# Attention feeding a gated FFN on one core: transposes and output products one slot later, three sets of exponentials, another order of the score tiles, an earlier load of q and k

## The chip, the cores and the metric

One Trainium2 chip, one of its cores. The metric is device time in microseconds (us) of one launch: the median of several runs. Instructions are named by engine: TensorE (PE in the profile; PEld is its weight load), VectorE (DVE), ScalarE (ACT), GpSimd (POOL), SyncE (SP, which here only issues DMAs).

## The reference

```python
def _attn_ref(q, k, v):                       # 8 x 8 heads, 576 positions, 64 wide
    scores = scale * np.matmul(q, k.transpose(0, 1, 3, 2))
    mask = block_i >= block_j                 # causal over blocks of 64
    scores = np.where(mask, scores, -1000000000.0)
    scores = scores - np.max(scores, axis=-1, keepdims=True)
    attn = np.exp(scores)
    attn = attn / (np.sum(attn, axis=-1, keepdims=True) + 1e-09)
    return np.matmul(attn, v).astype(np.float32)

def _moe_ref(x, w_a, w_b, w_out):             # x: 4608 x 512, w: 512 x 1536, 1536 x 512
    a = x @ w_a
    b = x @ w_b
    return (a * b @ w_out).astype(np.float32)
```

The attention's output, heads side by side, is x. The weights of the FFN come as 64-bit floats, and the kernel converts them to pairs of a high and a low 32-bit part; most matrix products are made of three products of such parts.

## The kernel before

The kernel has two stages. The first is the **attention loop**, a loop over *slots* s, one for each of the 64 heads and LAG = 2 more. In it the attention is the main thread, and a first pass of the FFN (features 0 to 3 of 12, `first_pass`) is strewn between its steps as *filler*: single matmuls of 288 columns (line 217). The second stage, behind the loop, does the other features (`pair_unit`, `pair_out`, lines 708 and 754), while VectorE converts their weights. The change touches nothing in the second stage.

Three generators make a head i:

- `softmax(i)`: a side block (line 412, 128 x 128) and four tiles of scores (line 392: `last`, of 512 columns, and t = 0, 1, 2 of 192, 320 and 448); VectorE masks them (lines 413, 414, 430) and takes the maxima (398, 420, 421); ScalarE makes the exponentials (line 401: `e`, and `e_s` of the side block) with their sums. The side block lies in the same PSUM tile as score tile 1 (`p1`), of which the pool `ps_sc` has three. A last step sums and inverts (lines 435 to 442, `rc`) and has GpSimd normalise the exponentials in place (line 445). The exponentials lie in NE = 2 sets of buffers, used in turn (`i % NE`).
- `turn(i)`: the transposes of the exponentials on TensorE in four steps, t = 3, 2, 1, 0 (line 468, `tp`), ScalarE's copy of each (line 470, `ah`) and VectorE's remainder (line 472, `al`).
- `values(i)`: the output products with v in two steps (lines 517 to 523, `av`), their sums (lines 527 to 532), and for every odd head the split of x into high and low parts (`xh`, `xl`).

The first 8 heads (NATIVE) use plain fp32 matmuls without the split into parts. A slot runs through a table of steps: which generator, for which head relative to s, and how many thirty-sixths of a slot's filler follow it. `now` is the slot number with that fraction. `want(now)` says how many filler matmuls are to be issued by then: it begins at MOE_FROM = 10.2 and reaches 36 a slot from slot 18 on. The conversion of the first pass's 12 weight parts (`convert_w`, lines 139 to 149 on VectorE, with ScalarE and GpSimd) is paced by `n_conv`: one part a slot, five steps each. `KEEP` adds idle matmuls in slots 0 and 1.

q and k of a pair of heads come by `load_pair` (lines 321 and 322, one buffer each behind the first four pairs), are scaled and split by `split_q` and `split_k`, and are spread to both halves of the partitions by four DMAs a head in `spread` (lines 358 and 359). All these are issued by SP in one queue, together with the loads of v (line 330), of weights (line 124), and the partial outputs (line 555).

The order in which an engine gets its instructions is not exactly that of the program: a scheduler takes, of those that it holds to be ready, the one that was written first. `behind_of` pins an instruction behind another in its queue, without a wait.

Of the kernel before, what the change touches and what calls it, by code (L numbers as in the profile page):

```python
# [23 lines left out]
CONV_PER_SLOT = 1.0  # L24
CONV0 = 1
HL_DVE = False
MOE_FROM = 10.2
# [6 lines left out]
NATIVE = 8  # L34
SPARE = 8
# [17 lines left out]
def attention_then_bilinear_ffn(  # L53
# [10 lines left out]
    nc = tc.nc  # L64
    B, H, D, S = kT.shape
# [217 lines left out]
    NE = 2  # L283
# [90 lines left out]
    def softmax(i):  # L374
# [51 lines left out]
        for t in range(LAST):  # L426
            ps = p1 if t == 1 else ps_sc.tile([P, 512], F32, tag="sc", name=f"s{t}{n}")
            mark = scores(t, ps)

            nc.vector.memset(ps[:BLK, nk[t] - BLK:nk[t]], NEG)  # L430
            top(t, ps[:, :nk[t]])
            exps(t, es[t][:, :nk[t]], ps[:, :nk[t]], nm[:, t:t + 1])
            if t < LAST - 1 or not native:
                yield mark
# [15 lines left out]
    def turn(i):  # L450
# [8 lines left out]
        for t in range(LAST, -1, -1):  # L459
# [14 lines left out]
            if t == SIDE_T and not native:  # L474
                yield mark
                behind_of(lower(), "rc")
                continue
            if not native:
                ins = lower()
                if t == 0:  # L480
                    behind_of(ins, "rc")
# [101 lines left out]
    def want(now):  # L583

        n = (now - H - LAG) * per_slot - behind
        if now < 2 * H + LAG:
            n = (H * per_slot - behind) * (now - MOE_FROM) / (2 * H + LAG - MOE_FROM)
        return int(n)
# [6 lines left out]
    SLOT = [(S_, 0, 3), (S_, -1, 0), (T_, -2, 4), (S_, 0, 4), (V_, -2, 3), (S_, 0, 3),  # L595
            (T_, -1, 4), (V_, -2, 3), (S_, 0, 3), (T_, -1, 5), (T_, -1, 4)]
    fill = sum(m for _, _, m in SLOT)
    gens = {}
    for s in range(NH + LAG):
        p, odd = divmod(s + 4, 2)  # L600
        if p < NH // 2 and not odd:
            load_pair(p)
# [3 lines left out]
        for what, i, m in SLOT:  # L606
            i += s
            if 0 <= i < NH:
                steps.append((gens.get((what, i)) or gens.setdefault((what, i), what(i)), m))
        due = k = 0  # L610
        for g, m in steps:
            mark = next(g)
# [5 lines left out]
            marks.append(mark)  # L618
            if k == 1 and 0 < s <= NH:
                split_v(s - 1)  # L620
# [4 lines left out]
            if k == (3 if odd else 6) and s + 2 < NH:  # L625
                spread(s + 2)
            k += 1
            due += m
            now = s + due / fill
            while n_conv < 5 * int(now * CONV_PER_SLOT + CONV0):  # L630
                next(conv, None)
                n_conv += 1
# [261 lines left out]
```

## Time and profile before

| | |
|---|---|
| median of 3 runs | 1279.61 us (1277.71 to 1281.69) |
| the profiled execution | 1281.83 us, its span 1279.8 us |
| TensorE matmul busy | 1239.3 us, 97% |
| TensorE weight load busy | 1173.2 us, 92% |
| VectorE busy | 999.2 us, 78% |
| ScalarE busy | 683.6 us, 53% |
| GpSimd busy | 554.9 us, 43% |
| granted TensorE clock, mean | 0.988 |

The attention loop ends about 640 us into the span. Busy times are shares of the whole; the two stages have different limits, so a stage has to be read by itself. Ends of matmuls are modelled, so that a TensorE that shows no idle time may still issue more slowly than it could; the length of a slot, from one head's side block to the next, is the safer measure. "A <- B: x, n, m" in the waits says that A stood idle for x us in all, n times, at most m, until B was done.

### The profile page before, as it was taken

The page shows a single profiled execution, that of the slowest core. Times are in us where ns is not written, and L with a number is a line of the kernel's source. Part 1 is how long each engine was busy: PE and PEld are TensorE (multiplying, and loading weights), DVE is VectorE, ACT ScalarE, POOL GpSimd, SP SyncE. Part 2 cuts the span into 40 slices and gives each one's busy share as a digit, 9 for nine tenths or more (in the row PEclk, how much of TensorE's full clock was granted, in tenths as well). Part 3 has the DMA queues.
Part 4 walks back from the last instruction along what each step waited for, and adds up shares of the span by engine and source line. Part 5 has one row for each costly group of instructions (what it writes and reads, how often), then busy time and mean ns, then how long its engine had stood idle before and what let it go on. Part 6 is the DMA issues. An engine that isn't in the chain of part 4 may idle for free.

```text
span 1279.8 us, 23524 instructions
## 1 busy us (share of the span) xinstructions
PE 1239.3 (97%) x7849; PEld 1173.2 (92%) x7849; DVE 999.2 (78%) x2389; ACT 683.6 (53%) x1722; POOL 554.9 (43%) x679
## 2 busy tenths in 40 slices
PE   9988999999999999999988998999999999999998
PEld 5668998999999999999988998999999999999998
DVE  6878887777887877877699999899967577577553
ACT  5788787788787788888745423233222222122210
POOL 4567565566665565665422322223223123123231
PEclk8999999999999999999998999999999999999999
DMA  5467766777767767676225355364466442243131
GB/s 195 132 167 201 187 174 175 178 171 181 170 167 179 179 171 176 167 178 155 87 94 171 100 180 194 139 206 164 141 220 244 145 149 79 70 149 98 52 99 62
DMA packets 93496, 196.58 MB, mean 154 GB/s; under 512 B 11968, under 2 KB 52928, under 8 KB 93376
## 3 DMA queue, kind: packets, MB, share of 16 engines
q1 hardware_dynamic: 88768, 185.64, 51.4%
q10 hardware_dynamic: 4608, 9.44, 2.0%
q8 instruction: 63, 1.03, 0.3%
q14 instruction: 57, 0.47, 0.1%
HBM read 96.47 MB, written 47.19 MB: 112 GB/s over the span
## 4 chain that ended last, share of the span: by engine, by line
PE 71%; DVE 15%; DMA 4%; issue 4%; ACT 3%; POOL 2%; SPq 1%; ACTq 0%; DVEq 0%; POOLq 0%
PE pso_z L754 13%; PE ps L217 12%; PE tp L468 7%; PE psx_z L708 6%; PE psw_z L708 6%; PE psv_z L708 6%; PE pso L217 4%; PE s L392 4%; PE psy_z L708 3%; PE av L517 3%; PE av L523 3%; PE sl L392 2%; DMA kp<-kT 2%; PE av L507 2%; DVE sw L147 1%
## 5 line engine op out<-in xcount | busy, mean ns | idle before, releaser
L113 POOL TENSOR_TENSOR h_z<-u_z,h_z 128x384 fp32r<-128x384 f32 x96 | 112.8, 1175 | 391.4 <-ACT h_z L110 379.8
L217 PE MATMUL ps<-xh,wab 128*128 128x288 f32 x1024 | 241.8, 304 | 1.2 <-ACT a L241 1.2
L754 PE MATMUL pso_z<-h_z,wo 128*128 128x384 f32 x1152 | 204.0, 335 | 4.5 <-POOL h_z L113 4.5
L445 POOL TENSOR_SCALAR e<-e,rc 128x512 f32<-128x512 f32 (+3 forms) x256 | 151.6, 604 | 127.9 <-DVE rc L442 118.1
L754 PEld LDWEIGHTS pso_z<-h_z,wo 128*128 128x128 f32 x1152 | 199.6, 188 | 7.0 <-POOL h_z L113 7.0
L217 PEld LDWEIGHTS ps<-xh,wab 128*128 128x128 f32 x1024 | 172.3, 189 | 4.7 <-ACT a L241 1.4
L472 DVE TENSOR_TENSOR al<-tp,ah 128x512 fp32r<-128x512 f32 x224 | 131.6, 608 | 31.5 <-ACT ah L470 31.0
L217 PE MATMUL ps<-xl,wab 128*128 128x288 f32 x512 | 154.1, 301 | 0.0
L468 PE MATMUL tp<-ident,e 128*128 128x128 f32 x832 | 136.1, 278 | 10.4 <-POOL e L445 4.0
L470 ACT CAST ah<-tp 128x512 fp32r<-128x512 f32 x224 | 116.4, 531 | 50.3 <-PE tp L468 47.5
L110 ACT CAST h_z<-u_z 128x384 fp32r<-128x384 f32 x96 | 49.3, 514 | 167.7 <-DVE u_z L733 160.2
L217 PE MATMUL pso<-hh,wo 128*128 128x288 f32 x512 | 128.1, 311 | 4.3 <-ACT hh L110 4.3
L708 PE MATMUL psx_z<-xh,wab 128*128 128x384 f32 x384 | 118.5, 344 | 7.2 <-DVE u_z L726 6.7
L468 PEld LDWEIGHTS tp<-ident,e 128*128 128x128 f32 x832 | 100.8, 142 | 25.7 <-POOL e L445 9.5
L401 ACT ACTIVATE e<-s,nm 128x192 f32<-128x192 f32 (+2 forms) x192 | 101.5, 529 | 32.4 <-DVE nm L398 23.2
L708 PE MATMUL psw_z<-xh,wab 128*128 128x384 f32 x384 | 117.0, 340 | 0.8 <-DVE u_z L728 0.8
L708 PE MATMUL psv_z<-xh,wab 128*128 128x384 f32 x384 | 116.7, 339 | 0.5 <-DVE u_z L730 0.4
L398 DVE TENSOR_REDUCE nm<-s 128x1 f32<-128x192 f32 (+3 forms) x256 | 109.9, 431 | 2.4
L217 PEld LDWEIGHTS ps<-xl,wab 128*128 128x128 f32 x512 | 96.5, 188 | 3.4
L217 PEld LDWEIGHTS pso<-hh,wo 128*128 128x128 f32 x512 | 88.3, 192 | 6.6 <-ACT hh L110 5.3
L113 POOL TENSOR_TENSOR v<-vr,v 128x320 fp32r<-128x320 f32 x56 | 50.2, 897 | 89.3 <-ACT v L110 67.9
L392 PE MATMUL s<-k,q 128*128 128x256 f32 x336 | 81.2, 322 | 2.2 <-ACT e_s L401 1.9
(142 smaller groups left out, 2919.5 us busy)
## 6 DMA issues: line engine op xcount, KB each, us to landing
k<-kp SPq DMA_DIRECT2D x112, 288.0 KB, 3.8
xr<-xd SPq DMA_DIRECT2D x48, 384.0 KB, 3.5
pt<-part SPq DMA_DIRECT2D x96, 192.0 KB, 3.5
q<-qp SPq DMA_DIRECT2D x112, 160.0 KB, 2.6
raww<-wab SPq DMA_DIRECT2D x24, 512.0 KB, 3.8
qp<-qT SPq DMA_DIRECT2D x32, 320.0 KB, 3.2
vr<-vm SPq DMA_DIRECT2D x64, 160.0 KB, 3.1
kp<-kT SPq DMA_DIRECT2D x32, 288.0 KB, 3.5
```

What stands on the lines that cost most here:

```text
L110: nc.scalar.copy(hi, src)
L113: return lo_eng.tensor_tensor(lo, src, f32(hi), op=ALU.subtract)
L217: mm = nc.tensor.matmul(ps, w_, d_, start=(i == 0), stop=(i == n - 1))
L392: mark = nc.tensor.matmul(ps[:, :w], qm[:, q0[t]:q0[t] + P], kk[:, :w], start=(i == 0), stop=(i == len(ks) - 1))
L398: nc.vector.tensor_reduce(nm[:, t:t + 1], view, axis=AX.X, op=ALU.max, negate=True)
L401: nc.scalar.activation(out, view, AF.Exp, bias=bias, accum_out=sm[:, t, :1])
L445: nc.gpsimd.tensor_scalar(ev, ev, rc[:, t:t + 1], 1.0, op0=ALU.mult, op1=ALU.mult)
L468: mark = nc.tensor.transpose(tp[:, c], src, ident)
L470: nc.scalar.copy(ah[:, :m, cols], tp[:, :m])
L472: return nc.vector.tensor_tensor(al[:, :m, cols], tp[:, :m], f32(ah[:, :m, cols]), op=ALU.subtract)
L708: nc.tensor.matmul(ps, wt[:, i, iw], j[:, ix], start=start and kp == 0 and i == 0 and j is xh, stop=kp == KP - 1 and i == 1, skip_group_ch ...
L754: nc.tensor.matmul(ps, wt[:, a, osl], b, start=i == 0, stop=i == 3 * len(fs) - 1)
```

## The change

- From slot SW = 10 on another table of steps holds: all four transposes of head s − 2, and the output products of head s − 3. Before, three of the four transposes were those of head s − 1, and the products those of head s − 2. The loop has one slot more. Slots 0 to 9 keep the old table, with the first transpose and the second step of the output products exchanged.
- Three sets of exponentials instead of two.
- The score tiles come in the order last, 1, 0, 2 (before: last, 0, 1, 2), and from slot 10 on the steps of `softmax` stand 10, 7, 10 and 9 thirty-sixths apart (before 7, 7, 10 and 12).
- VectorE's remainders of the transposes are no longer pinned behind the sums (`rc`).
- The filler's pace is shifted by FFLAG = 3 slots in place of LAG = 2.
- The weight conversion goes at 0.7 parts a slot in the first 8 slots and 0.9 behind (before 1).
- `load_pair` is called in the middle of the odd slot before, instead of at the start of the even one; `split_v` a slot later.
- The scratch that GpSimd's DMAs would use is smaller.

```diff
-CONV_PER_SLOT = 1.0
+SW = 10
+FFLAG = 3.0
...
-    NE = 2
+    NE = 3
...
-        for t in range(LAST):
+        for t in (1, 0, 2):
             ps = p1 if t == 1 else ps_sc.tile([P, 512], F32, tag="sc", name=f"s{t}{n}")
...
-            if t == SIDE_T and not native:
-                yield mark
-                behind_of(lower(), "rc")
-                continue
             if not native:
-                ins = lower()
-                if t == 0:
-                    behind_of(ins, "rc")
+                lower()
             yield mark
...
-        n = (now - H - LAG) * per_slot - behind
-        if now < 2 * H + LAG:
-            n = (H * per_slot - behind) * (now - MOE_FROM) / (2 * H + LAG - MOE_FROM)
+        n = (now - H - FFLAG) * per_slot - behind
+        if now < 2 * H + FFLAG:
+            n = (H * per_slot - behind) * (now - MOE_FROM) / (2 * H + FFLAG - MOE_FROM)
...
-    SLOT = [(S_, 0, 3), (S_, -1, 0), (T_, -2, 4), (S_, 0, 4), (V_, -2, 3), (S_, 0, 3),
-            (T_, -1, 4), (V_, -2, 3), (S_, 0, 3), (T_, -1, 5), (T_, -1, 4)]
+    SLOT1 = [(S_, 0, 3), (S_, -1, 0), (T_, -2, 4), (S_, 0, 4), (V_, -2, 3), (S_, 0, 3),
+             (V_, -2, 3), (T_, -1, 4), (S_, 0, 3), (T_, -1, 5), (T_, -1, 4)]
+    SLOT = [(S_, 0, 3), (S_, -1, 0), (T_, -2, 4), (V_, -3, 3), (S_, 0, 3), (T_, -2, 4), (S_, 0, 3),
+            (V_, -3, 3), (T_, -2, 4), (S_, 0, 4), (T_, -2, 5)]
...
-    for s in range(NH + LAG):
-        p, odd = divmod(s + 4, 2)
-        if p < NH // 2 and not odd:
-            load_pair(p)
+    for s in range(NH + LAG + 1):
+        odd = s % 2
+        if s == 0:
+            load_pair(2)
...
-        for what, i, m in SLOT:
+        for what, i, m in SLOT if s >= SW else SLOT1:
...
-            if k == 1 and 0 < s <= NH:
-                split_v(s - 1)
+            if k == 1 and 0 < s - (s >= SW) <= NH:
+                split_v(s - 1 - (s >= SW))
...
+            if odd and k == 5 and s + 5 < NH:
+                load_pair((s + 5) // 2)
...
-            while n_conv < 5 * int(now * CONV_PER_SLOT + CONV0):
+            while n_conv < 5 * int(CONV0 + 0.7 * min(now, H) + 0.9 * max(now - H, 0)):
...
-    nc = bacc.Bacc("TRN2", target_bir_lowering=False, num_devices=1)
+    nc = bacc.Bacc("TRN2", target_bir_lowering=False, num_devices=1, dynamic_dma_scratch_size=1024)
```

`split_v` is called for the head one further back from slot 10 on. In slots where a generator has nothing left to do (at the change-over), its step issues nothing.

More of the change, by code (lines that the diff above doesn't have):

```diff
@@ L611, in attention_then_bilinear_ffn @@
         for g, m in steps:
-            mark = next(g)
+            mark = next(g, None)
             if not m:
@@ L617, in attention_then_bilinear_ffn @@
                 nc.tensor.matmul(keep, z[:, :P], z, start=True, stop=True)
-            marks.append(mark)
-            if k == 1 and 0 < s <= NH:
-                split_v(s - 1)
+            if mark:
+                marks.append(mark)
+            if k == 1 and 0 < s - (s >= SW) <= NH:
+                split_v(s - 1 - (s >= SW))
             if k == (3 if odd else 4) and s + 2 < NH:
```

## The prediction

> **What bounds the kernel now.** I read the page's first two parts, then the busy time of each engine slot by slot (a slot is one turn of the attention loop), then the waits, then the order of time inside two slots.
>
> ```profile
> span 1279.8 us, 23524 instructions
> PE 1239.3 (97%) x7849; PEld 1173.2 (92%) x7849; DVE 999.2 (78%) x2389; ACT 683.6 (53%) x1722; POOL 554.9 (43%) x679
> PE   9988999999999999999988998999999999999998
> DVE  6878887777887877877699999899967577577553
> PEclk8999999999999999999998999999999999999999
> ```
>
> TensorE is the bound nearly everywhere; only holes in its work can be won. The attention loop takes the first 20 of the 40 slices, and the change touches nothing behind it. So the question is how large the holes in the loop are. The slot starts (first side matmul, line 412) cut the steady part into even and odd slots of equal TensorE work. The next two rows are sums over 20 even slots (217.85 to 598.98) and the 20 odd ones between and behind them:
>
> ```profile
> sum 199.90, PE 198.10 PEld 186.66 DVE 173.34 ACT 163.82 POOL 156.53; mean PE 9.90 PEld 9.33 DVE 8.67 ACT 8.19 POOL 7.83
> ...
> sum 190.77, PE 190.77 PEld 186.22 DVE 136.02 ACT 149.23 POOL 82.50; mean PE 9.54 PEld 9.31 DVE 6.80 ACT 7.46 POOL 4.13
> ```
>
> The same matmuls take 10.00 us in an even slot and 9.54 in an odd one. I take 9.54 as TensorE's floor, since there it is never idle. The early slots, one row each, and rows that cover several, the last of them behind the loop:
>
> ```profile
> 19.72:34.81 15.09, 15.09 (x62) 9.93 (x61) 9.70 (x26) 9.08 (x26) 9.68 (x10) 0.55 0.34 108
> 42.75:54.40 11.65, 10.38 (x59) 6.80 (x58) 10.86 (x29) 8.41 (x24) 8.58 (x11) 0.85 0.57 159
> 70.82:78.60 7.78, 7.78 (x55) 5.58 (x55) 6.26 (x20) 6.86 (x20) 4.49 (x6) 1.00 0.56 191
> ...
> 106.45:119.03 12.58, 9.98 (x68) 8.64 (x67) 11.47 (x32) 8.84 (x25) 7.63 (x10) 1.00 0.73 176
> ...
> 194.78:208.29 13.51, 11.63 (x72) 10.75 (x71) 8.63 (x26) 9.09 (x26) 7.12 (x10) 0.87 0.65 172
> ...
> 6.01:97.00 90.99, 84.12 (x493) 57.01 (x492) 73.82 (x206) 66.13 (x181) 54.38 (x65) 0.91 0.55 162
> 97.00:146.77 49.77, 46.46 (x324) 42.55 (x323) 44.13 (x130) 40.94 (x112) 35.50 (x47) 1.00 0.70 191
> 97.00:175.71 78.71, 74.18 (x520) 68.47 (x518) 68.40 (x204) 63.63 (x177) 51.81 (x71) 1.00 0.71 189
> ...
> 700.00:900.00 200.00, 190.93 (x1065) 183.91 (x1065) 188.35 (x328) 70.06 (x120) 54.24 (x41) 1.00 0.51 169
> ```
>
> Columns: stretch and length, then busy time of TensorE, its weight loads, VectorE, ScalarE, GpSimd, granted clock, DMA share, GB/s. The reader is to see VectorE nearly as busy as the slot is long in 42.75 and 106.45, and the halved clock in 19.72.
>
> **The change, part by part.**
>
> *Transposes and output a slot later, three sets of exponentials (from slot 10).* In even slots TensorE waits for normalised exponentials and for the copied transposes. From the waits between 150 and 600 us:
>
> ```profile
> PE tp L468 <- POOL e L445: 1.4, 1, 1.4
> PEld av L517 <- ACT ah L470: 3.3, 20, 0.2
> ```
>
> Behind the change head i's transposes are issued in slot i+2 and its output products in slot i+3, so both inputs are about 0.6 to 0.9 slots (6 to 8 us) older when they are asked for. Both waits then have no place, and nor has the long one in slot 20. The 20 even slots give 199.90 − 190.77 = 9.1 us; slot 20 gives 13.51 − 9.54 = 4.0 us, its halved clock included. Together −13.1. What is late next is the score tile below. The third set costs three small GpSimd memsets at the start, under the first wait for q; the matmuls are the same.
>
> *Score tiles in the order last, 1, 0, 2.* Tile 1 shares its PSUM tile with the side block and waits until the side block's exponential (e_s) is done. It comes second now instead of third. An even slot and an odd slot, from the order of time:
>
> ```profile
> 413.65 0.34 PE L412 MATMUL s<-k,q 128*128 128x128 f32 x2
> 414.34 0.29 PE L217 MATMUL ps<-xh,wab 128*128 128x288 f32 x1
> 414.47 0.30 PE L217 MATMUL ps<-xl,wab 128*128 128x288 f32 x1
> 417.64 0.45 PE L392 MATMUL s<-k,q 128*128 128x320 f32 x2
> 416.69 0.37 ACT L401 ACTIVATE e_s<-s,nb 128x128 f32<-128x128 f32 x1
> ...
> 423.47 0.33 PE L412 MATMUL s<-k,q 128*128 128x128 f32 x2
> 427.15 0.45 PE L392 MATMUL s<-k,q 128*128 128x320 f32 x2
> 425.69 0.37 ACT L401 ACTIVATE e_s<-s,nb 128x128 f32<-128x128 f32 x1 [0.34 <-DVE nb L421]
> ```
>
> The slots begin with the side block at line 412. A filler matmul takes 0.13 us (414.34 to 414.47). In the odd slot e_s is done 2.59 us into the slot and tile 1 starts at 3.68; in the even one 3.41 and 3.99. Ahead of tile 1 there stand now 14 fillers, two transposes, a score tile and four output products. After the change there stand 10 fillers, four transposes and the same four products; two transposes more and a score tile less about cancel, so it is due 4 × 0.13 us sooner, at 3.1 to 3.2 us. With e_s at 2.59 nothing waits; at 3.41 TensorE would wait 0.3 to 0.4. Which of them holds is not in the trace: the even slots are late because the x split of an odd head and two late remainders of transposes run at their start, and with output a slot later that split falls at the start of odd slots, and the last transpose's remainder there is a small one. Ends: 0, and 0.4 in each of some 45 slots, 18 us. I take 2 us, near the odd row, because what made the even row late is partly gone.
>
> *Weight conversion slower in the first eight slots (0.7 parts a slot instead of 1), 0.9 behind.* By the pacing formula the 12 parts are now due at slots 0 to 11, and then at 0, 1.4, 2.9, 4.3, 5.7, 7.1, 8.4, 9.6, 10.7, 11.8, 12.9, 14.0. VectorE's five steps of the 11 parts before 97 us:
>
> ```profile
> L145 DVE SCALAR_TENSOR_TENSOR mw<-raww,mw 128x512 f32<-128x512 uint16 x11 | 9.6, 868 | 0.2
> L149 DVE TENSOR_TENSOR xw<-mw,sw 128x512 f32<-128x512 f32 x11 | 9.2, 841 | 0.5
> L147 DVE SCALAR_TENSOR_TENSOR sw<-raww,sw 128x512 int32<-128x512 int32 x11 | 8.6, 782 | 0.7 <-ACT sw L140 0.6
> L143 DVE TENSOR_SCALAR mw<-raww 128x512 int32<-128x512 int32 x11 | 8.5, 776 | 0.0
> L139 DVE TENSOR_SCALAR sw<-raww 128x512 int32<-128x512 int32 x11 | 5.6, 513 | 0.1
> ```
>
> A part costs 868 + 841 + 782 + 776 + 513 ns = 3.8 us. Slots 0 to 9 have 8 parts instead of 11, VectorE 11 us less there. TensorE lacks work for 90.99 − 84.12 = 6.9 us in that stretch and runs some 14 us at half clock (15.09 us at 0.55), which is 7 us more. Ends: −10, if the early waits that ruin the clock go, and +2, if the new order adds a wait. The first part and the first head's normalisation, which stand in front of the first hole, are unmoved, and slot 7 (70.82) is TensorE's own already. I take −3.
>
> *The change-over at slot 10.* Slots 10 to 14 get the three parts back, 11.3 us by those durations, and lose one head's transposes and outputs to later slots. VectorE's rows of these, 97 to 147 us:
>
> ```profile
> L472 DVE TENSOR_TENSOR al<-tp,ah 128x512 fp32r<-128x512 f32 x16 | 10.7, 673 | 1.1 <-ACT ah L470 1.0
> L532 DVE TENSOR_TENSOR xf<-av,avlo 64x512 f32<-64x512 f32 x5 | 3.4, 677 | 0.1
> L531 DVE TENSOR_TENSOR avlo<-avlo 64x64 f32<-64x64 f32 x5 | 3.2, 630 | 1.3 <-ACT avlo L530 1.2
> L472 DVE TENSOR_TENSOR al<-tp,ah 128x256 fp32r<-128x256 f32 x5 | 2.1, 415 | 0.0
> ```
>
> A head has 3 × 673 + 415 + 677 + 630 ns = 3.7 us of them. So VectorE has 44.1 + 11.3 − 3.7 = 51.7 us in slots 10 to 14. TensorE has less than before: the filler starts at 10.2 with 240 matmuls over 8.8 slots (27.3 a slot) instead of 7.8 (30.8). Its floor: a steady slot is 9.54, of which 36 × 0.131 = 4.7 is filler, leaving 4.8 for attention; five slots with 131 fillers make 5 × 4.8 + 131 × 0.131 = 41.2, less some 3.4 for the head that moved (24 of a slot's 34 attention matmuls), 37.8 us. VectorE becomes the bound of these slots and leaves TensorE 13.9 us without work; the buffers let it work ahead a little, and I take 13 up to slot 18. Before, the eight slots 10 to 17 (24 + 7 × 31 fillers by the old pace) had a floor of 70.2 us and took 78.71, holes of 8.5. The difference is +4.5. Ends: −2, if the extra slot of slack lets TensorE run ahead, and +10, if the clock falls as well.
>
> It can fall. The stretches around the wait in slot 20:
>
> ```profile
> 198.00:201.40 3.40, 1.75 (x11) 1.28 (x9) 2.67 (x8) 2.39 (x8) 2.48 (x2) 1.00 0.30 101
> 201.40:204.80 3.40, 3.17 (x13) 3.13 (x14) 1.05 (x4) 1.47 (x4) 2.04 (x5) 0.50 0.95 196
> ```
>
> TensorE was busy 1.75 of 3.40 us, and the next 3.40 us ran at 0.50: half idle was enough, and it cost 1.7 us. [...] The trace shows the fall after a half idle window, so I keep +10.
>
> *q and k loaded half a slot sooner.* The load is issued by SP, and SP holds it until the single buffer is free, that is, until the spreading DMAs of the pair before have landed (SP's own waits, 150 to 620 us):
>
> ```profile
> SPq L322 <- DMA q<-qp: 33.5, 25, 3.3
> SPq L321 <- DMA k<-kp: 10.5, 11, 1.9
> ```
>
> Asking sooner doesn't free the buffer, so 0. If the load's place in SP's queue shifts, a v load or a partial output behind it moves by at most the 3.3 us above, which the added slot covers.
>
> *One more slot, and the rest.* The filler's pace is shifted by the same slot (FFLAG), so the same 1968 filler matmuls are issued at the end of the loop, and the weights of the second stage find their memory free at the same point of TensorE's work: 0, with ±1.5 for a stage that VectorE's 188.35 of 200 us show to be close (row from 700 to 900). No DMA is issued by GpSimd, so its smaller scratch costs nothing.
>
> **Sum.** −13.1 + 2 + 4.5 − 3 + 0 = −9.6 us. The profiled execution took 1281.83 us (2.0 outside the span), so 1272.2 on its scale; the median of the runs is 2.2 below it, 1279.61, so **1270 us** on the median's.
>
> **The rivals.**
>
> *Tile 1 waits in every slot (slower).* The four-tile transpose now early in each slot puts a copy on ScalarE and a subtraction on VectorE ahead of e_s. If e_s is ready 0.4 to 0.5 us too late in all 45 slots, the 2 us become some 20: 1270 − 2 + 20 = 1288. It decides for slower from a mean wait of about 0.35 us. For it: the even slots' 3.41 against 3.1. Against it: e_s's chain is emitted ahead of the transpose, and odd slots have 0.5 us to spare. Chance 0.12.
>
> *The change-over eats the gain (no change, or little).* VectorE's 51.7 us plus two or three half-clock windows makes +12 instead of +4.5: 1277.5. For it: slot 11 with one part took 12.58 us at 11.47 of VectorE. Against it: the transposes behind it have a slot of slack. Chance 0.15.
>
> *The early clock holds (much faster).* With VectorE free of 11 us the holes that halve the clock in 20 to 34 us go: −11 instead of −3, 1262. Against it: the first hole's cause is unmoved. Chance 0.12.
>
> *The change does nothing in the steady slots:* the scheduler that orders each queue packs the later work just as tightly, and another wait of half a microsecond takes the place: 1279.6. Chance 0.05.
>
> **How the numbers follow.** My forecast has 0.56, with 1264 to 1276 as its own range (−13.1 to −7 steady, −2 to +10 at the change-over, −6 to +1 early, not all at one end). The range 1261 to 1282 takes in the second to fourth rival and leaves out the first. About 0.3% (3.8 us) is what a measurement of this kernel can tell from no change. Faster: 0.51 of the forecast, 0.12, and 0.05 of the change-over's, 0.68. Same: 0.05 + 0.08 + 0.05 = 0.18. Slower: 0.12 and 0.02 of the change-over's, 0.14.
>
> **What would show it.** Even and odd slots both at 9.5 to 9.6 us from slot 20 on; no wait of transposes for GpSimd's e or of output products for ScalarE's ah there; tile 1 starting near 3.1 us with e_s done before it. Slots 10 to 14 with VectorE over 90% busy, four weight parts and TensorE idle for 10 us or more. A shorter stretch before slot 10 with fewer weight steps. The stage behind the loop as long as before. The prediction is wrong if tile 1's start is pinned to the end of e_s in most slots, if the slots 10 to 14 hold no hole, or if the half-clock stretch at 20 us is gone.

## Result and the profile after

The changed kernel takes 1288.25 us in the median (1286.6 to 1293.92), the kernel before 1279.57 (1276.81 to 1281.69) beside it: a ratio of 1.0081 (95% interval 1.0062 to 1.01). It is slower by 8.7 us; 1270 was forecast, in a range of 1261 to 1282. The profiled execution took 1288.09 us. Two of the ten executions of E2 below took 2383 and 3046 us, and the only trace of E2 is of the second, so E2 has a time (the median of all ten) and no slots. The page of the changed kernel:

```profile
span 1285.9 us, 23499 instructions
PE 1231.5 (96%) x7849; PEld 1170.3 (91%) x7849; DVE 1006.2 (78%) x2389; ACT 690.8 (54%) x1723; POOL 555.7 (43%) x684
...
PE   8989899999999999999998998999999999999998
...
PEclk9999999999999999999998999999999999999999
```

The matmuls are the same 7849, TensorE is busy 8 us less (less time at half clock: the granted clock is 0.995 in the mean instead of 0.988) and the span is 6.1 us longer: more holes. Four stretches of the span add up to it. Of the kernel before (the first two of its stretches, 90.99 and 78.71 us, stand in the prediction) from slot 18 to the last output product, and from there to the end; and of the changed kernel from slot 0, 10, 19 and the last output product on:

```profile
175.71:639.38 463.67, 459.64 (x3303) 440.80 (x3302) 361.31 (x1144) 366.53 (x1026) 277.10 (x398) 1.00 0.67 167
639.38:1279.80 640.42, 616.77 (x3534) 603.80 (x3532) 494.69 (x836) 185.85 (x337) 170.22 (x132) 0.99 0.42 138
```

```profile
6.01:85.88 79.87, 74.37 (x492) 52.35 (x492) 70.47 (x199) 63.93 (x179) 51.50 (x63) 1.00 0.61 180
85.88:173.53 87.65, 77.68 (x531) 72.05 (x530) 75.25 (x227) 69.63 (x194) 56.57 (x79) 0.98 0.71 191
173.53:645.26 471.73, 457.61 (x3286) 437.82 (x3285) 364.74 (x1128) 369.90 (x1015) 275.34 (x393) 1.00 0.62 162
645.26:1285.90 640.64, 617.31 (x3538) 604.92 (x3537) 494.81 (x836) 185.84 (x337) 170.66 (x132) 0.99 0.42 138
```

Slots 0 to 9: −11.1 us. The change-over (eight slots before, nine now, with the same filler): +8.9. The rest of the loop: +8.1. The second stage: +0.2. What the early slots win is nearly given back by slot 19; the loss is made in the steady slots, where 11 us were to be won. Of the change-over, slots 10 to 14, which were to hold the most of VectorE's work:

```profile
85.88:134.86 48.98, 42.76 (x286) 38.93 (x284) 42.43 (x129) 38.35 (x105) 33.28 (x45) 0.97 0.69 194
```

The sums over the even slots 20 to 58 and the odd ones 21 to 59:

```profile
sum 207.73, PE 196.61 PEld 186.73 DVE 166.29 ACT 176.40 POOL 135.96; mean PE 9.83 PEld 9.34 DVE 8.31 ACT 8.82 POOL 6.80
```

```profile
sum 197.05, PE 194.38 PEld 186.80 DVE 150.44 ACT 144.26 POOL 104.30; mean PE 9.72 PEld 9.34 DVE 7.52 ACT 7.21 POOL 5.22
```

An even slot takes 10.39 us instead of 10.00, an odd one 9.85 instead of 9.54: now the odd slots lose too. The waits between 180 and 610 us name two things, tile 1 (line 393) behind e_s, and ScalarE behind q's load:

```profile
PE s L393 <- ACT e_s L402: 12.1, 29, 1.0
PEld s L393 <- ACT e_s L402: 20.6, 33, 1.3
ACT qp L338 <- DMA qp<-qT: 12.7, 12, 1.9
```

The last was 0.3 us in two times before. How the two hang together shows in the order of time around the start of slot 52, at 505.83 us, the longest of the steady slots (11.37 us); first ScalarE, then VectorE, then TensorE:

```profile
505.71 0.74 ACT L338 ACTIVATE qp<-qp 128x640 fp32r<-128x640 f32 x1 [1.86 <-DMA qp<-qT]
506.48 0.59 ACT L472 CAST ah<-tp 128x512 fp32r<-128x512 f32 x1
506.96 0.67 ACT L345 CAST kp<-kp 128x576 fp32r<-128x576 f32 x1
...
510.18 0.37 ACT L402 ACTIVATE e_s<-s,nb 128x128 f32<-128x128 f32 x1 [0.54 <-DVE nb L422]
```

```profile
507.10 0.69 DVE L474 TENSOR_TENSOR al<-tp,ah 128x512 fp32r<-128x512 f32 x1 [2.08 <-ACT ah L472]
507.70 0.61 DVE L399 TENSOR_REDUCE nm<-s 128x1 f32<-128x448 f32 x1
508.27 0.42 DVE L474 TENSOR_TENSOR al<-tp,ah 128x256 fp32r<-128x256 f32 x1
508.70 0.11 DVE L414 MEMSET s<- 64x64 f32 x1
...
508.92 0.62 DVE L399 TENSOR_REDUCE nm<-sl 128x1 f32<-128x512 f32 x1
509.47 0.27 DVE L399 TENSOR_REDUCE nm<-s 128x1 f32<-128x128 f32 x1
509.77 0.15 DVE L421 TENSOR_REDUCE nb<-nm 64x2 f32<-64x2 f32 x1
509.93 0.15 DVE L422 TENSOR_REDUCE nb<-nm 64x2 f32<-64x4 f32 x1
```

```profile
505.83 0.33 PE L413 MATMUL s<-k,q 128*128 128x128 f32 x2
...
507.93 0.63 PE L470 MATMUL tp<-ident,e 128*128 128x128 f32 x4 [0.86 <-DVE al L474]
...
510.69 0.56 PE L393 MATMUL s<-k,q 128*128 128x320 f32 x2 [0.52 <-ACT e_s L402]
```

ScalarE stands 1.86 us for q's load in front of the split of q; behind it waits the copy `ah` of tile 1's transpose; VectorE stands 2.08 us for that copy, because the remainder `al` of tile 1 is next in its queue, and then runs the remainder of tile 0 as well, all ahead of the maximum over the new head's `sl` (3.09 us into the slot; 0.88 in slot 47 of E11 below, where neither remainder is in front of it). So `nb`, e_s and tile 1 are late; tile 1 starts at 510.69, 0.14 us after e_s. TensorE stands twice in this slot: 0.86 us ahead of a transpose, until a remainder has freed the PSUM tile `tp`, and 0.52 us for e_s. In most of the other slots only the wait for e_s is there. In the kernel before both remainders were pinned behind `rc`, which comes after `nb`.

### The profile page after: what moved, and what is told of

Same layout as the page of the kernel before. It is cut to its first block, busy times and chain, and to the rows that moved or that the text cites. A ratio compares the mean times of both kernels' runs of the same rounds, so it can differ in the third digit from the quotient of the medians.

```text
span 1285.9 us, 23499 instructions
## 1 busy us (share of the span) xinstructions
PE 1231.5 (96%) x7849; PEld 1170.3 (91%) x7849; DVE 1006.2 (78%) x2389; ACT 690.8 (54%) x1723; POOL 555.7 (43%) x684
## 4 chain that ended last, share of the span: by engine, by line
PE 50%; DVE 19%; DMA 15%; ACT 7%; issue 5%; SPq 3%; POOL 1%; ACTq 0%; DVEq 0%; POOLq 0%
PE pso_z L756 14%; PE psx_z L710 6%; PE psw_z L710 6%; DMA k<-kp 6%; PE psv_z L710 6%; DMA kp<-kT 5%; PE ps L218 5%; PE psy_z L710 3%; PE tp L470 3%; DVE nm L399 3%; PE s L393 3%; PE pso L218 2%; DVE al L474 2%; DVE sw L148 2%; SPq L359 2%
## 5 line engine op out<-in xcount | busy, mean ns | idle before, releaser
L218 PE MATMUL ps<-xh,wab 128*128 128x288 f32 x1024 | 237.5, 301 | 0.0
L447 POOL TENSOR_SCALAR e<-e,rc 128x512 f32<-128x512 f32 (+3 forms) x256 | 162.9, 649 | 109.4 <-DVE rc L444 89.2
L474 DVE TENSOR_TENSOR al<-tp,ah 128x512 fp32r<-128x512 f32 x224 | 138.5, 619 | 29.5 <-ACT ah L472 27.5
L218 PE MATMUL ps<-xl,wab 128*128 128x288 f32 x512 | 156.9, 306 | 0.3 <-POOL xl L114 0.3
L470 PE MATMUL tp<-ident,e 128*128 128x128 f32 x832 | 133.5, 275 | 7.1 <-POOL e L447 2.5
L472 ACT CAST ah<-tp 128x512 fp32r<-128x512 f32 x224 | 119.3, 533 | 23.2 <-PE tp L470 20.2
L218 PE MATMUL pso<-hh,wo 128*128 128x288 f32 x512 | 120.3, 303 | 3.9 <-ACT hh L111 3.9
L393 PE MATMUL s<-k,q 128*128 128x320 f32 (+1 forms) x336 | 86.0, 337 | 19.1 <-ACT e_s L402 18.1
L114 POOL TENSOR_TENSOR hl<-hf,hh 128x288 fp32r<-128x288 f32 x64 | 54.5, 851 | 81.5 <-ACT hh L111 81.4
```

Of the source, the lines that this page charges most:

```text
L114: return lo_eng.tensor_tensor(lo, src, f32(hi), op=ALU.subtract)
L218: mm = nc.tensor.matmul(ps, w_, d_, start=(i == 0), stop=(i == n - 1))
L393: mark = nc.tensor.matmul(ps[:, :w], qm[:, q0[t]:q0[t] + P], kk[:, :w], start=(i == 0), stop=(i == len(ks) - 1))
L447: nc.gpsimd.tensor_scalar(ev, ev, rc[:, t:t + 1], 1.0, op0=ALU.mult, op1=ALU.mult)
L470: mark = nc.tensor.transpose(tp[:, c], src, ident)
L472: nc.scalar.copy(ah[:, :m, cols], tp[:, :m])
```

## Experiments

Times are medians; each ratio is to the kernel before, measured beside it on the same chip. "Mean" is the mean length of slots 19 to 62 in the profiled execution, and "nb" the median over these slots of the time from the slot's start to the end of `nb`; both are of one execution. Two versions that were not measured side by side are best compared by the ratio and the mean: the difference of their medians is good to a few microseconds only (the kernel before came to 1278.3 to 1280.5 us beside them).

| kernel | time, us | ratio (95%) | mean, us | nb, us |
|---|---|---|---|---|
| before | 1279.6 | 1 | 9.84 | 2.13 |
| after | 1288.3 | 1.0081 (1.0062 to 1.01) | 10.09 | 2.91 |
| E1 after, tiles last, 0, 1, 2 | 1293.3 | 1.0103 (1.0062 to 1.0143) | 10.08 | 3.53 |
| E2 before, tiles last, 1, 0, 2 | 1280.5 | 1.0001 (0.9976 to 1.0026) | – | – |
| E3 after, conversion at 1 part | 1301.5 | 1.017 (1.0125 to 1.0216) | 10.01 | 2.90 |
| E4 before, conversion at 0.7 and 0.9 | 1279.9 | 1.0 (0.9981 to 1.0019) | 9.86 | 2.13 |
| E5 after, load at the old place | 1290.7 | 1.0078 (1.0056 to 1.01) | 10.07 | 2.90 |
| E6 after, side block with tile 0 | 1290.4 | 1.0079 (1.0051 to 1.0106) | 10.08 | 3.33 |
| E7 after, old order and spacing | 1287.0 | 1.0052 (1.0037 to 1.0068) | 9.84 | 2.99 |
| E8 after, x split a step later | 1289.1 | 1.0075 (1.0053 to 1.0097) | 10.05 | 2.91 |
| E9 after, tile 0's remainder put off | 1295.3 | 1.0125 (1.0103 to 1.0147) | 10.41 | 2.45 |
| E10 old table a slot later, pins | 1288.8 | 1.0102 (1.0045 to 1.016) | 9.95 | 2.60 |
| E11 E10 and splits pinned | 1274.9 | 0.9933 (0.9902 to 0.9965) | 9.64 | 2.13 |
| E12 new spacing, pins | 1302.6 | 1.0195 (1.0146 to 1.0245) | 10.36 | 2.12 |
| E13 after, splits pinned | 1284.8 | 1.0041 (1.0019 to 1.0062) | 10.00 | 2.63 |
| E14 before, splits pinned | 1277.6 | 0.9978 (0.9965 to 0.9991) | 9.65 | 2.12 |
| E15 E1 and splits pinned | 1290.2 | 1.0073 (1.0049 to 1.0097) | 10.00 | 3.01 |
| E16 E7 and splits pinned | 1279.3 | 0.9986 (0.9965 to 1.0007) | 9.87 | 2.72 |
| E17 E11 without the pins of the remainders | 1289.0 | 1.009 (1.0056 to 1.0125) | 10.03 | 2.98 |
| E18 before without these pins | 1323.3 | 1.0339 (1.0308 to 1.0369) | 10.60 | 3.27 |

**E1, E2: the order of the tiles.**

```diff
-        for t in (1, 0, 2):
+        for t in range(LAST):
```

> The changed kernel with the old order of the score tiles (last, 0, 1, 2). Theory A (tile 1, now second, waits for the side block's exponential e_s because both lie in one PSUM tile): tile 1 is due near 5 us of a slot instead of 3.1, e_s is long done; slots 19 to 62 go from 10.09 us to 9.6, and the time from 1288 to about 1267. Theory B (the steps of older heads crowd VectorE and ScalarE, whatever the tile order): the slots stay near 10.1 and the time near 1288. Theory C (late loads of q and k hold ScalarE): only part comes back, every fourth slot stays above 10.3, about 1278.

> The kernel before with only the score tiles' order changed to last, 1, 0, 2. Theory A: tile 1 is due near 1.8 to 2.3 us of a slot and e_s is done at 2.6 (odd slots) and 3.4 (even slots), so TensorE waits some 0.7 to 1.4 us in each of 55 slots; less the old holes, 1305 to 1330. Theory B or C: within 3 us of 1279.6.

 (the same line the other way round, in the kernel before)

The order was not the cause. In E1 TensorE's matmuls wait for e_s no more, and the mean is the same 10.08: the holes stand in front of the output products and the next score tiles instead. In the kernel before, the new order does not change the time.

```profile
PE av L513 <- ACT ah L472: 6.5, 20, 0.5
PE s L393 <- ACT e L402: 2.5, 3, 1.7
```

**E6: the side block in tile 0's PSUM tile**, so that tile 1 owes e_s nothing.

```diff
-        side = p1[:, nk[1]:nk[1] + P]
+        side = p1[:, 256:256 + P]
...
-            ps = p1 if t == 1 else ...
+            ps = p1 if t == 0 else ...
```

> The changed kernel in the new order (last, 1, 0, 2), but the side block lies in tile 0's PSUM tile instead of tile 1's; nothing else moves. Theory A: tile 1 has no one to wait for, tile 0 comes third, near 5 us, behind e_s; about 1267, as in the run with the old order. Theory B: near 1288, since the order and the work are the same.

Mean 10.08, waits of transposes in place of tile 1's. With E1: take tile 1's wait away, and the next thing that TensorE asks for waits.

**E3, E4: the pace of the conversion**, in the changed kernel and in the kernel before.

```diff
-            while n_conv < 5 * int(CONV0 + 0.7 * min(now, H) + 0.9 * max(now - H, 0)):
+            while n_conv < 5 * int(now + CONV0):
```

> The changed kernel with the weights converted at the old pace, 1 part a slot. If the slower pace is what brings slot 10 from 97.0 to 85.9 us: slot 10 back near 94 to 97 us, slot 19 later than 173.5 by less than that, since the conversion is over sooner, and the time 1286 to 1292 us (0 to 3 of it kept). Rival 'the early gain is that of the third set of exponentials and of the loads': slot 10 stays at 86 to 89 us. In both the steady slots stay at 10.05 to 10.1 us, since no part of the conversion runs there.

> The kernel before with one part of the change alone: the weights converted at 0.7 part a slot in the first eight slots and 0.9 after, instead of 1. Theory 'the slower conversion is worth the whole early gain': slot 10 starts near 86 instead of 97.0 us, no half-clock stretch is left before 60 us, and the time is 1279.6 - 11 = about 1269 us (ratio 0.991). Rival 'the early gain came from the new order of loads and the extra set of exponentials': slot 10 stays near 97 us and the time within 0.3% of before. Second rival, 'the conversion comes back later': slots 10 to 25 hold more conversion and give back 4 or more of the 11 us, 1273 to 1276 us.

E3 (slot 0 to 10, slot 10 to 19), then E4 (slot 0 to 10, slot 10 to 18):

```profile
5.60:96.63 91.03, 81.52 (x492) 56.06 (x492) 74.33 (x212) 67.53 (x185) 57.37 (x65) 0.93 0.58 170
96.63:185.07 88.44, 77.90 (x531) 72.11 (x530) 70.31 (x215) 67.16 (x186) 53.17 (x77) 0.98 0.69 177
```

```profile
6.01:93.36 87.35, 84.09 (x492) 55.96 (x492) 68.10 (x200) 63.72 (x178) 46.28 (x61) 0.98 0.55 162
93.36:174.35 80.99, 74.26 (x519) 68.65 (x518) 71.12 (x210) 65.96 (x182) 56.37 (x75) 1.00 0.70 188
```

In the changed kernel the slower pace is worth 13 us by the medians and 11 by the ratios: with the old one slot 10 starts at 96.6 us again, and the change-over is no shorter. In the kernel before it wins only 3.6 us by slot 10, 1.4 of them are left at slot 18, and the time is the same: its theory fell. The other early 7 us come from the rest of the change or from the clock, which fell early in some executions and not in others: E15 and E16 have the slower pace too and differ from each other only from slot 10 on; up to there E15 ran at a clock of 0.90 and E16 at 0.98, and they began slot 10 at 92.52 and 87.74 us. Which part of the rest was not tried.

**E5, E8: the load and the x split.** E5 calls `load_pair` at the start of the even slot again. E8 puts a `yield` ahead of the split of an odd head's x and a step `(V_, -4, 0)` at the head of the table.

> The changed kernel with q and k loaded at the old place (start of the even slot). Theory C: ScalarE's waits for q's DMA (12.7 us in 180 to 610 us of the changed kernel) shrink to about 1, the slots with the longest holes (every fourth) lose some 0.6 us each, about 1281. Theory A: the load is gated by its single buffer, not by its place, so the time stays within 3 us of 1288.

> The changed kernel with the split of a pair's x (two copies of ScalarE, two subtractions of GpSimd and the store's issue on ScalarE) moved from the end of the output's second step to the start of the next slot, ahead of the side matmul. Theory 'x split': ScalarE's copies of x and the issue behind them delay e_s and the copies ah in each odd slot; moved away, odd slots lose 0.2 to 0.4 us, and the time comes to 1277 to 1283 us. Rival (pins, or the load that ScalarE waits for): odd slots stay within 0.1 us of 10.0 and the time at 1285 to 1292 us.

Neither changes anything: the load as the prediction had it (ScalarE's wait for q is 12.7 us, as after), and the theory of the x split falls.

**E7: the old order and spacing**, transposes and output still a slot later.

```diff
-        for t in (1, 0, 2):
+        for t in range(LAST):
...
+    SLOT = [(S_, 0, 3), (S_, -1, 0), (T_, -2, 4), (S_, 0, 4), (V_, -3, 3), (S_, 0, 3),
+            (T_, -2, 4), (V_, -3, 3), (S_, 0, 3), (T_, -2, 5), (T_, -2, 4)]
```

> The changed kernel with the old table of the slot and the old order of the tiles, only with every transpose at head s-2 and every output step at head s-3. Theory 'spacing': what makes the steady slots 10.1 us is that the last score tile, two transposes and the output's second step now stand close together at the slot's end; with the old spacing and the later heads the steady slots come to 9.6 to 9.85 us and the time to 1266 to 1277 us. Rival 'crowded queues whatever the spacing' (the remainder of the transposes of tile 1 and tile 0, no longer pinned behind the reciprocals, stands ahead of the maximum over the last score tile on VectorE, and ScalarE stops in its order at q's load): slots of 10.0 to 10.2 us and 1284 to 1295 us, whatever the table.

The mean is that of the kernel before, 9.84, so 0.25 us a slot belong to order and spacing together. It is not what the later transposes were to bring, `nb` is as late as in the changed kernel, and the time hardly moves: slot 19 begins 5.5 us later than in the changed kernel (179.02 against 173.53 us).

**E9, E12: the pins with the new spacing.** E9 puts off tile 0's remainder alone (a step `(T_, -3, 0)` behind `rc`). E12 has the `turn` of the kernel before, with its two pins, and the changed table with `(T_, -3, 4)` as its first transpose, so that tile 0's transpose falls at the start of the next slot.

> The changed kernel with the remainder of tile 0's transpose (VectorE, 128x256) put off to the next slot and pinned behind the reciprocals again, as in the kernel before; the remainder of tile 1 stays where the change put it. Theory 'pins': this remainder no longer stands ahead of the maximum over the last score tile; e_s's end comes 0.3 to 0.4 us sooner in a slot, tile 1's wait goes, and the time falls by 8 to 16 us to 1272 to 1280 us. Rival (the delay comes from ScalarE's queue, or from the spacing): the wait moves to another releaser and the time stays at 1284 to 1292 us.

> The changed kernel with its own order of tiles and its own spacing, but the transposes one step further on, so that tile 0's falls at the start of the next slot, and the remainders of tile 1 and tile 0 pinned behind the reciprocals as in the kernel before. Theory 'pins': the reduction over the two maxima ends at 2.1 us of a slot again instead of 2.8, e_s at 2.6 instead of 3.4, tile 1 (due at 3.15) waits in no slot, steady slots of 9.6 to 9.7 us, time 1268 to 1274 us. Rival 'spacing' (the last score tile a twelfth of a slot later, two transposes close behind it): slots stay at 10.0 or above and the time at 1284 to 1292 us.

E12 is half right: `nb` ends at 2.12 us again and tile 1 waits no more. But in the new spacing the first output step stands directly behind tile 0's transpose, and TensorE's only wait is this one:

```profile
PE av L519 <- ACT ah L472: 22.8, 39, 1.9
```

So with this table the pins cost more than they win. The splits of q and k (below) are not pinned in E12, whose slots of number 2 modulo 4 take 11.29 us and the others 9.97 to 10.09; new spacing, pins and pinned splits together were not run. E9 came out above both of its ranges: `nb` ends at 2.45 us, but the waits for e_s stay (13.4 us in 14 times). That the remainder, put off, also holds its transpose's PSUM tile longer may be why; it is not shown.

**E10, E11, E13, E14: the splits of q and k.** E10 is the changed kernel with order, spacing, pins and place of tile 0's transpose of the kernel before, all a slot later (`T_` at −3 and −2, `V_` at −3). In E11, E13 and E14 the two ScalarE copies are pinned behind e_s of the even slot:

```diff
-        exps(NT, e_s, side, nb[:, 1:])
+        last["es"] = exps(NT, e_s, side, nb[:, 1:])
...
-        nc.scalar.mul(qp[:, 1].bitcast(F32R), qp[:, 0], SCALE)
+        behind_of(nc.scalar.mul(qp[:, 1].bitcast(F32R), qp[:, 0], SCALE), "es")
...
-            nc.scalar.copy(kp[:, 0].bitcast(F32R), kp[:, 1])
+            behind_of(nc.scalar.copy(kp[:, 0].bitcast(F32R), kp[:, 1]), "es")
```

> The changed kernel with the slot of the kernel before in all but the one thing: order of tiles last, 0, 1, 2, the old spacing, tile 0's transpose at the start of the next slot, and the remainders of tile 1 and tile 0 pinned behind the reciprocals; transposes and output stay one slot later, with three sets of exponentials. Theory 'the slot later is right, what was moved along with it costs': the slots whose number is a multiple of 4 fall from 10.4 to 9.7 us, the others stay at 9.55 and 9.85, the mean comes to about 9.65, and the time to 1279.6 - 8 = 1272 us (1268 to 1276). Rival 'one slot later is itself the cost' (GpSimd's normalisation and the transposes of an older head meet the new head's work): slots of 10.0 us and more, 1284 us or above. Third, the output's later start is paid back in the change-over: 1277 to 1283 us with a steady mean under 9.75.

> The changed kernel with one order added on ScalarE: its two copies that split a pair's q and k (0.74 and 0.67 us, in the changed kernel at 9 us of an odd slot to 1 us of the next, where ScalarE stops for q's load for 1 us at a time) come behind e_s of the even slot. Theory 'splits at the boundary': these copies and the wait in front of them are what makes e_s end at 3.4 us in the slots that follow them; the wait of ScalarE for q's load goes from 12.7 us in all to under 2, slots of number 0 and 2 modulo 4 fall from 10.47 and 10.19 to about 9.9, the odd ones stay at 10.05 and 9.65, mean 9.85 to 9.95, and the time falls by 6 to 10 us to 1278 to 1282 us. Rival 'the queues are full whichever work stands there': the wait moves, slots stay at 10.05 or above, 1285 us or more.

> The kernel of 'table of before, one slot later' (1288.8 us), with the same order added: the copies that split q and k on ScalarE behind e_s of the even slot. In that kernel nearly all that TensorE loses in steady slots stands before the first transposes of every second or fourth slot, behind ScalarE's wait for q's and k's loads. Theory 'splits at the boundary': these holes go, slots of number 2 modulo 4 fall from 10.63 to 9.7, the mean from 9.95 to 9.65 or less, and the time to 1272 to 1278 us, which would be less than the kernel before. Rival 'full queues': mean above 9.85 and 1284 us or more.

> The kernel before with the same order added: here the two copies stand at 6.4 and 8.6 us of an odd slot, and go to some 3 us of the next. If the later place is free in itself: 1277 to 1281 us. If loads and spreads then come too late for the next pair, or e_s's neighbours on ScalarE are delayed: 1283 us or more, and then the place behind e_s costs in the other two kernels too.

E10 fell: a slot later, with the changed kernel's earlier load, slower conversion and third set, brought nothing. The split of q began 6.4 us after the start of an odd slot before (median), and 9.1 in the changed kernel, close to the next slot's start; pinned, it begins 3.2 to 3.3 us into the even slot. The spacing moved it, and not the load: E1 and E7 differ in the spacing alone and have it at 10.1 and 7.2 us, and E5, with the load at the old place, at 9.2. E13 won 3.4 us, less than expected. E11 won 13.9 us over E10 by the medians (1.7% by the ratios, 14.0 us in the 44 steady slots), as expected, and is the fastest version of all (its trace is of an execution of 1281.07 us, with slot 10 at 94.9 us). E14 came out a little faster than the kernel before too. Slots 19 to 62 in the kernel before, E14 and E11, one row of each:

```profile
185.25:618.10 432.85, 429.17 (x3083) 411.61 (x3082) 339.42 (x1078) 344.48 (x969) 260.52 (x374) 1.00 0.68 170
```

```profile
187.80:612.33 424.53, 423.73 (x3083) 409.39 (x3081) 349.23 (x1078) 345.66 (x969) 262.79 (x374) 1.00 0.68 174
```

```profile
180.92:604.85 423.93, 422.09 (x3083) 409.59 (x3082) 347.16 (x1079) 346.64 (x969) 261.94 (x375) 1.00 0.68 175
```

E14's transposes are as early as ever, and its steady slots are as short as E11's.

**E15, E16, E17, E18: what is left, and the pins alone.** E15 and E16 are E1 and E7 with the splits pinned. E17 is E11, and E18 the kernel before, without the pins of the remainders:

```diff
-            if t == SIDE_T and not native:
-                yield mark
-                behind_of(lower(), "rc")
-                continue
...
-                ins = lower()
-                if t == 0:
-                    behind_of(ins, "rc")
+                lower()
```

> The changed kernel with two things undone together: the order of tiles (last, 0, 1, 2, so that tile 1 comes in the middle of the slot) and the place of the splits of q and k (pinned behind e_s of the even slot). Each alone left the steady slots at 10.08 and 10.00 us. Theory 'two waits behind one another, each hidden by the other': with both gone the mean comes to 9.65 to 9.75 and the time to 1268 to 1276 us. Rival 'the new spacing and the remainders that are no longer pinned': the mean stays at 9.85 to 10.0, 1280 to 1287 us, with e_s's wait replaced by waits of transposes or of the output.

> The changed kernel with the old order of tiles, the old spacing (transposes and output a slot later, tile 0's transpose still at the slot's end) and the splits of q and k pinned behind e_s; the remainders of tile 1 and tile 0 on VectorE stay free, as the change left them. Against the kernel of 1274.9 us (slots of 9.64) it differs in these remainders and in tile 0's place alone. Theory 'the splits alone were left': mean 9.6 to 9.7, 1271 to 1278 us. Rival 'the free remainders cost': the reduction nb ends at 2.6 us or later in most slots, mean 9.75 to 9.9, 1279 to 1286 us.

> The kernel of 1274.9 us (table of before one slot later, splits of q and k behind e_s; slots of 9.64) with one thing taken out: VectorE's remainders of tile 1 and tile 0 are no longer pinned behind the reciprocals but issued at once, as in the changed kernel. Tile 0's transpose stays at the start of the next slot. Theory 'free remainders cost': the remainder of tile 1 (0.69 us) stands ahead of the maximum over the last tile at the slot's start again, nb ends at 2.6 us or later in many slots, mean 9.8 to 9.9, 1280 to 1286 us. Rival 'only the place of tile 0's transpose counted': mean 9.6 to 9.7 and 1272 to 1278 us.

> The kernel before with one part of the change alone: VectorE's remainders of tile 1 and tile 0 are issued at once and no longer pinned behind the reciprocals. Theory 'the pins are the step that I costed at nothing': the remainder of tile 1 (0.67 us) stands ahead of the maximum over the last score tile at the slot's start, nb ends near 2.9 us instead of 2.13 in most slots, odd slots leave their floor of 9.54, the mean goes from 9.84 to 10.0 to 10.2 us, and the time to 1286 to 1296 us. Rival 'the pins matter only once transposes and output come a slot later': mean within 0.05 of 9.84 and time within 0.3% of before.

E15's first theory fell: with the new spacing and free remainders the mean stays at 10.0. In E16 the rival held (1279.3 us, 9.87 a slot). E17 shows what the free remainders cost, more than I expected: it differs from E11 in them alone and takes 14.1 us more by the medians, 10.03 against 9.64 us a slot (17 us over the 44 slots). `nb` ended within 2.2 us in 31 of E11's 44 slots, and in none of E17's. VectorE at the start of slot 46 of E17 (445.80 us), then of slot 47 of E11 (452.08 us):

```profile
446.32 0.69 DVE L474 TENSOR_TENSOR al<-tp,ah 128x512 fp32r<-128x512 f32 x1 [0.65 <-ACT ah L472]
447.02 0.11 DVE L414 MEMSET s<- 64x64 f32 x1
447.05 0.62 DVE L399 TENSOR_REDUCE nm<-sl 128x1 f32<-128x512 f32 x1
...
447.77 0.41 DVE L474 TENSOR_TENSOR al<-tp,ah 128x256 fp32r<-128x256 f32 x1
...
448.64 0.15 DVE L422 TENSOR_REDUCE nb<-nm 64x2 f32<-64x4 f32 x1
```

```profile
452.96 0.69 DVE L399 TENSOR_REDUCE nm<-sl 128x1 f32<-128x512 f32 x1
...
454.05 0.15 DVE L422 TENSOR_REDUCE nb<-nm 64x2 f32<-64x4 f32 x1
...
454.81 0.19 DVE L444 RECIPROCAL rc<-rc 128x5 f32<-128x5 f32 x1
454.92 0.98 DVE L474 TENSOR_TENSOR al<-tp,ah 128x512 fp32r<-128x512 f32 x2
```

In E17 the large remainder, and VectorE's 0.65 us of standing for its copy, come ahead of the maximum over `sl`, and the small one ahead of `nb`; in E11 both come behind `rc`. TensorE's own loss in E17 is at another place than tile 1:

```profile
PE tp L470 <- DVE al L474: 7.4, 19, 1.7
```

Its transposes wait until a remainder has freed a PSUM tile, and its matmuls wait for e_s only once (0.4 us; its weight loads 3.9 us in 13 times). So E17 shows that the free remainders cost, and not that they cost by way of `nb`. E18 did worse than I expected, 43 us instead of 6 to 16: with its early transposes the late `rc` (done 4.45 us into the slot in the median, 3.31 in the kernel before) makes GpSimd's normalised exponentials late too, a hole in nearly every slot. TensorE and its weight load, 180 to 630 us:

```profile
PE tp L468 <- POOL e L445: 26.2, 42, 0.9
PEld tp L468 <- POOL e L445: 35.7, 42, 1.1
```

## Why the prediction was wrong

- **Steady slots: −13.1 + 2 forecast; +11 came** (44 slots of 10.09 instead of 9.84). This is the step that failed, and no one term of it alone. The sum had no term for the pins of the remainders on VectorE, which the change lets go: they stood at nothing, without a cover being named. E18 prices this edit alone at +43 us in the kernel before, and E17 at +14 with later transposes; in the changed kernel itself their share was not measured, since put back there (E9, E12) they came with other holes. The new spacing was counted only through tile 1, in the +2: the old order and spacing (E7) take 0.25 us off each slot, 11 us in all, with the remainders still free. And the −13.1 does not come from the later transposes (third point). I read the odd slot's 2.59 us for e_s as a property of the slot; it was one of the pins (3.73 in the median slot of E18).
- **"What is late next is the score tile."** The place was right, and tile 1's due time too (3.13 to 3.15 us in slots without a hole; 3.1 to 3.2 forecast). Its size was wrong: the +2 was taken near the odd row, because "what made the even row late is partly gone". e_s ended at 3.38 us in the median slot. The rival *Tile 1 waits in every slot* gave 1288 for this at a chance of 0.12, and 1288.25 came, by luck, since the terms beside it were off too (−11.1 for −3 in the early slots). Of the copy and the subtraction that it feared early in the slot, the copy does stand ahead of e_s on ScalarE (in slot 47, from 454.84 us on, it is at 456.92 and e_s at 457.85), but e_s waits for `nb` (13.0 us in 31 times), which is late by the remainders of the slot's end. And E1 shows that without tile 1 another instruction would have waited for as long.
- **The even slots' 9.1 us were put down to early transposes.** Of the waits that the prediction names, the one that recurs comes to 3.3 us, not 9.1. E14 moves no transpose and brings the steady slots to 9.65, by moving two ScalarE copies; E10 moves transposes and output and leaves 9.95. So those waits were the last link and not the cause: the gap between even and odd slots lay in ScalarE's order. With both pins, E11 reaches 9.64, the length the prediction had in mind. What a later slot adds to E14 in the steady slots is 0.6 us over 44 slots, in the two rows above.
- **Weight conversion: −3 forecast, −11.1 came,** the lower end's cause and size: no half-clock stretch is left before slot 10 (79.87 us at a clock of 1.00). The edit was rightly tied to the early slots: E3 gives all of it back. I gave that end a chance of 0.12 because the first hole's cause is unmoved; a hole is still there (2.39 us busy of 3.41, last section), but the clock does not fall behind it; in the kernel before it fell behind 2.34 of 3.41 (17.07 to 20.48 us). The full size is in part the luck of one execution: with the same pace and the same early steps E15 ran at a clock of 0.90 up to slot 10 and E16 at 0.98, and slot 10 began 4.8 us later in E15.
- **Change-over: +4.5 forecast.** +8.9 came; 1.4 of it is one more slot of attention (4.8 us) less the head that moved (3.4), so +7.5 compares. It is within the ends (−2 to +10), with slot 14 at 13.14 us and the half clock that I had kept the end for. The mechanism came out only in part. Over slots 10 to 14 VectorE was busy 42.43 of 48.98 us, 87%, where 51.7 were forecast, and TensorE stood for 6.2 us, not 13.9. So VectorE did not become the bound of these slots, and that the size lay within the ends is in part luck. Early slots and change-over together gave −3.6 instead of +1.5, so they are not why the time rose.
- **Load of q and k: 0, right** (E5). But the load's wait mattered in another way: the scheduler put the split that needs it in front of tile 1's copy, and at slot 52 ScalarE stood 1.86 us for the load before it ran either. I counted SP's queue and not ScalarE's.
- **The second stage: 0, right** (640.42 and 640.64 us).
- **Scheduler packs as tightly** ("the change does nothing in the steady slots", 0.05) came nearest to what E1, E6 and E15 show: taking away one wait uncovers the next.

Still open: how the 0.45 us a slot between the changed kernel and E11 divides into order, spacing, pins and splits. They do not add: the splits' pin is worth 0.09 (E13), −0.03 (E16), 0.32 (E11) and 0.19 (E14) a slot. Why the new spacing moves the split of q was not tried by itself.

## What to carry to other kernels

An ordering pin that the diff deletes is an instruction moved: ask what its queue will run instead at the moment that the bottleneck's next input is made, and price that with the rows of that queue. A wait at the end of a chain (transposes waiting for a copy) does not say that this chain is too short; first look at what its engine was doing in the 2 us ahead of it. Where several queues meet at one point of the loop, undoing one cause showed little or nothing here (E1 and E6 10.08 us a slot, E13 10.00, against 10.09); take the best arrangement and put the suspects back one at a time (E17).

## What the runs showed of the hardware

Around the start of slot 52 of the changed kernel ScalarE stood 1.86 us for a load, and the copy next in its queue, whose transposes had ended at 503.65 us, began at 506.48; VectorE stood 2.08 us for that copy, and TensorE in the end: tile 1 started 4.86 us into the slot instead of 3.14, and 0.86 us of that were a wait for a transpose's PSUM tile, 0.52 us one for e_s.

The clock: in the trace of the changed kernel and in that of the kernel before it changes only at multiples of 3.41 us from its other changes (in the changed kernel it falls at 132.40, 695.59 and 1006.21 us), so stretches are cut on that grid here. In the changed kernel, one with TensorE busy for 0.32 us was followed by 0.50, and two with 2.39 and 1.73 us were not:

```profile
23.17:26.58 3.41, 2.39 (x16) 1.74 (x17) 3.18 (x14) 3.16 (x12) 3.10 (x6) 1.00 0.46 154
26.58:29.99 3.41, 3.41 (x34) 3.02 (x32) 3.35 (x9) 2.87 (x6) 1.46 (x1) 1.00 0.23 68
...
129.00:132.40 3.40, 0.32 (x2) 0.32 (x3) 1.29 (x5) 2.09 (x5) 1.39 (x2) 1.00 0.46 157
132.40:135.80 3.40, 3.40 (x16) 3.27 (x15) 2.83 (x9) 3.09 (x11) 3.39 (x7) 0.50 0.65 138
...
166.53:169.95 3.42, 1.73 (x13) 1.72 (x14) 3.23 (x10) 2.77 (x8) 2.40 (x2) 1.00 0.11 29
169.95:173.36 3.41, 3.03 (x22) 2.75 (x21) 3.11 (x9) 2.92 (x9) 2.90 (x6) 1.00 0.95 203
```

The prediction's stretch (1.75 us busy, 1.77 on the grid) was followed by 0.50, the one here with 1.73 was not. On that grid eight stretches at full clock in these two traces were followed by half clock: TensorE was busy for 0.32, 1.42 and 1.60 us in those of the changed kernel, and for 2.34, 2.14, 1.77, 1.61 and 1.32 us in those of the kernel before. All 726 others were followed by full clock, 19 of them with 1.67 to 2.44 us busy; so half idle was not enough each time, and the busy time alone does not tell here behind which stretch the clock fell. (Busy time rests on modelled ends of matmuls.)
